# Carried state multiplied without a block copy, two more units with an early bonus, and a new order of all steps

## The chip, the cores and the metric

The kernel runs on one core of one Trainium2 chip. The metric is the device time of one execution in microseconds (us); the median of several runs counts. The core's engines are TensorE (PE in the profile; its weight loads are PEld), VectorE (DVE), ScalarE (ACT) and GpSimd (POOL); SyncE (SP) issues the DMAs.

## The reference

Three stages follow one another. A recurrence over time for 4 batches and 8 heads with a state of 48x48, then a feed-forward block with a softmax-weighted hidden layer and a layer norm, then a gated feed-forward block:

```python
for t in range(S):                       # B=4, H=8, S=768, D=48
    cur = einsum('bhd,bhe->bhde', u[None] * kt, vt)
    y[:, :, t] = einsum('bhd,bhde->bhe', rt, state + cur)
    state = wt[:, :, :, None] * state + einsum('bhd,bhe->bhde', kt, vt)
...
h = x @ w_in                             # 3072 x 384 -> 1024
e = exp(h - max(h)); solu = h * e / (sum(e) + 1e-9)
ln = (solu - mean(solu)) / sqrt(var(solu) + 1e-6) * g_ln
x = ln @ w_out                           # 1024 -> 384
...
gate = 1 / (1 + exp(-(x @ w_gate))); val = x @ w_val   # 384 -> 1536
out = (gate * val) @ w_out2              # 1536 -> 384
```

## The kernel before

**Units.** The recurrence is cut in 24 units, 6 chunks of 128 time steps for each batch. Within a unit the running product of the decay w (two scans, `sn1` and `sn2`, with the turn `cl` between them) scales r and k in place (`qm0`, `qm1`); `q` is the tile of scaled r and k. Then PE makes the scores of the chunk (`sco`, tile `pa`), a masked copy puts them into `a` (`mk0`, `mk1`) over a diagonal that holds the bonus term r·(u k) (`dg0`, `dg1` on POOL). The unit's output is two products that add up in one PSUM tile `py` (`out`): `a` times `v`, and the scaled r times the state that is carried in. The state is `yd` = old state + k·v (`new`, PE, then `yd`, DVE) and `xd` = `yd` times the decay `sc` (`scp` and `xd`). The first unit of a batch has no carried state, so 20 units have the second product. In the kernel before, `xb0` and `xb1` copy the two halves of `xd` into the tile `xblk`, whose other blocks stay zero, and the second product takes `xblk` as its weights, over all 112 rows.

**The bonus.** For units 0 to 2 it is one product in the layout of the scores (`rkp`) and four small matmuls against `u_blk` (`eb`, `ebc`). For the other units, r and k are loaded a second time in natural layout (`rk`), multiplied on POOL or DVE (`ru0`, `ru1`) and summed on DVE (`bon`).

**The feed-forward stages.** `g1a` to `g1c` are the first matmul of a unit (tile `ph`), `mx`, `ex`, `he`, `vs`, `rs0`, `rs1`, `no` the softmax and the norm, `zt` the transposes, `zh` and `zl` a high and a low part of the result, `g2` the second matmul (12 records a step; two steps a block of 128 columns for a pair of units), `xc` its copy. `g3g`, `g3v`, `ga`, `gm`, `gh`, `gl2`, `g4` are the gated block, whose PE work fills the time from about 385 us on. Weights arrive as 64-bit words and are decoded on DVE (`ci`, `co`, `wd`), with range watches on ACT (`ciw`, `cow`, `ww`); for units 0 to 2 the first matmul uses the plain decoded tile, from unit 3 on a high and a low part (`cih`, `cil`, `coh`, `col`).

**What sets the order.** The steps stand in a table, `ORDER`, in the order in which they are issued; each engine runs its own instructions in that order, and waits where data or a buffer is late. A suffix a, v or p puts a step on ACT, DVE or POOL. SP issues all loads in the table's order as well.

```python
    def step(name):
        name, _, at_ = name.partition(".")
        by = dict(by=at_[-1]) if at_[-1] in engines else {}
        ops[name](*map(int, at_.strip("avp").split(":")), **by)
```

Of the kernel before, what the change touches and what calls it, by code (L numbers as in the profile page):

```python
# [38 lines left out]
w.0 q.0 id.0 w.1 ub.0 mk.0 in_.0 q.1 sn1.0 v.0 in_.1 wo.0 cl.0 rkp.0p u.0 sn2.0 gl.0 q.2 qm0.0p in_.2 eb.0:0 v.1 v.2 ebc.0v sn1.1 qm1.0p sq.0 dg0.0  # L39
ktr.0:1 kcp.0 dg1.0 ciw.0 scp.1v cl.1 sco.0:2:3 w.2 ci0.0 sn2.1 rkp.1p q.3 new.0:4 eb.1:0 mk1.0 qm1.1p ebc.1 rk.3 sq.1 yd.0 mk0.0 dg0.1 ci1.0 out.0:1  # L40
dg1.1 ciw.1 ci0.1 v.3 ci1.1 xy.0 ci2.0 xm.0 qm0.1 cih.0 xd.0 ktr.1:0 ci2.1 xb1.0a kcp.1 sco.1:3:4 cow.0 cil.0v wo.1 mk0.1 rkp.2p mk1.1 cih.1 co0.0
eb.2:2 cow.1 co0.1 rk.4 cil.1v co1.0 ebc.2 ciw.2 dg0.2 new.1:1 dg1.2 yd.1 co2.0 ci0.2 cog.0 sn1.2 xb0.0 coh.0 out.1:0 ci1.2 scp.2 qm0.2p w.3 xy.1 v.4
ru0.3 q.4 g1a.0 xd.1 xm.1 ru1.3 cl.2 xb1.1a xb0.1 ci2.2 g1b.0 sn2.2 cih.2 g1c.0 cil.2v qm1.2p sq.2 cow.2 sco.2:3:4 mx.0 ru0.4 ktr.2:2 mk1.2 ex.0 ru1.4
mk0.2 sn1.3 out.2:1 kcp.2 rs0.0 cow.3 he.0 scp.3 new.2:0 qm0.3p w.4 v.5 xy.2 bon.3 q.5 g1a.1 vs.0 cl.3 xm.2 dg0.3 co1.1 dg1.3 rk.5 rs1.0 g1b.1 sn2.3
no.0 g1c.1 co0.2 qm1.3p sq.3 bon.4 zt1.0:4 co1.2 dg1.4 rk.6 zt0.0:3 zh1.0 ktr.3:2 zh0.0 dg0.4 sco.3:1:4 kcp.3 sn1.4 cl.4 scp.4 qm0.4p w.5 mx.1 sn2.4
ex.1 ru0.5v qm1.4p sq.4 yd.2 new.3:3 he.1 ru1.5 sco.4:2:0 rs0.1 xd.2 vs.1 g1a.2 ru0.6 mk1.3 yd.3 xb0.2 rs1.1 xb1.2a mk0.3 ktr.4:4 xd.3 g1b.2 kcp.4
ru1.6 co2.1 xb1.3a xb0.3 no.1 wl.0 new.4:3 sn1.5 out.3:1 cog.1 co0.3 qm0.5p coh.1 bon.5 v.6 xy.3 zt0.1:4 co1.3 dg1.5 rk.7 g1c.2 zh0.1 xm.3 dg0.5 scp.5
co2.2 g2.0 w.6 q.6 co2.3 cog.2 col.0v col.1 zt1.1:1 coh.2 cog.3 col.2 cl.5 zh1.1 ww.0 g2.1 mk0.4 sn2.5 mk1.4 qm1.5p xc.0 bon.6 out.4:4 sq.5 yd.4 rk.8
ru0.7v xd.4 ru1.7 coh.3 w.7 sn1.6 v.7 sco.5:1:2 xb1.4a xy.4 dg0.6 q.7 xm.4 dg1.6 g2.2 col.3 cl.6 g2.3 mx.2 qm0.6p sn2.6 ex.2 ru0.8v rs0.2 sq.6 qm1.6p
he.2 xc.1 g2.4 ru1.8 sn1.7 vs.2 ktr.6:0 wl.1 rs1.2 g2.5 kcp.6 mk0.5 xb0.4v scp.7 no.2 bon.7 qm0.7p w.8 mk1.5 rk.9 sco.6:3:4 xh.3 wd0.0 xc.2 xl.3  # L50
new.6:0 xh.4 out.5:1 mk1.6 xl.4 yd.6 xd.6 mk0.6 xy.5 dg1.7 q.8 zt1.2:2 cl.7 v.8 g1a.3 zh1.2 dg0.7 xm.5 xb1.6a ww.1 sn2.7 g1b.3 q.9 sn1.8 qm1.7p g1c.3
ru0.9 sq.7 ktr.7:4 mx.3 ru1.9 zt0.2:0 kcp.7 zh0.2 sco.7:3:1 scp.8 zl1.2 ex.3 qm0.8p w.9 zl0.2 out.6:4 mk0.7 xh.5 rs0.3 xb0.6 he.3 xl.5 new.7:2 xy.6
v.9 wd1.0 xm.6 vs.3 g1a.4 yd.7 rs1.3 bon.8 g1b.4 xd.7 rk.10 dg0.8 sn1.9 xb0.7 no.3 g1c.4 dg1.8 xb1.7a zt0.3:0 mx.4 xh.6 qm0.9p zt1.3:3 zh0.3 zh1.3
zl0.3 xl.6 ex.4 cl.8 g2.6 ru0.10 zl1.3 he.4 scp.9 g2.7 ru1.10 sn2.8 vs.4 g1a.5 wd2.0 qm1.8p xc.3 sq.8 g2.8 w.10 ktr.8:4 cl.9 wh.0 g1b.5 sn2.9 kcp.8
rs0.4v g2.9 qm1.9p sq.9 mk1.7 bon.9 bon.10 rs1.4 rk.11 ktr.9:2 xc.4 wlo.0 g1c.5 rk.12 kcp.9 no.4 g2.10 sn1.10 zt1.4:0 cl.10 scp.10 zt0.4:3 w.11 zh1.4
mx.5 ru0.11 g2.11 zh0.4 zl1.4 ru1.11 ex.5 sn2.10 sco.8:4:1 ru0.12 xc.5 new.8:2 ru1.12 out.7:0 he.5 rs0.5 sq.10 dg1.9 q.10 mk0.8 v.10 vs.5 g1a.6 dg0.9
wd0.1 xy.7 zl0.4 rs1.5 g1b.6 xm.7 yd.8 bon.11 no.5 sn1.11 g1c.6 rk.13 qm0.10p mk1.8 zt0.5:4 mx.6 zt1.5:0 zh0.5 sco.9:3:2 zh1.5 zl0.5 xh.7 wd1.1 ex.6
xl.7 new.9:1 out.8:4 rs0.6 ru0.13 he.6 xy.8 v.11 g2.12 dg1.10 q.11 xm.8 dg0.10 zl1.5 vs.6 g1a.7 cl.11 wd2.1 rs1.6 g2.13 no.6 qm1.10 g1b.7 mk0.9
qm0.11p xc.6 bon.12 xh.8 zt1.6:4 mk1.9 wh.1 rk.14 g2.14 xl.8 sn2.11 zh1.6 g1c.7 xd.8 qm1.11p sq.11 zl1.6 g2.15 wlo.1 xb0.8 scp.11 xb1.8a w.12 ru0.14
w.13 ktr.10:0 xc.7 zt0.6:3 g2.16 zh0.6 mx.7 zl0.6 ex.7 out.9:2 ru1.13v kcp.10v rs0.7 he.7 xy.9 dg1.11 q.12 sco.10:4:3 v.12 dg0.11 yd.9 vs.7 xm.9  # L60
sn1.12 new.10:0 sco.11:2:1 rs1.7 sn1.13 g1a.8 no.7 g2.17 qm0.12p mk0.10 mk1.10 cl.12 zt0.7:4 xc.8 sn2.12 g1b.8 zh0.7 mk1.11 qm1.12p sq.12 zt1.7:3
mk0.11 g1c.8 xd.9 zh1.7 xh.9v xb0.9 yd.10 xl.9 xb1.9a ktr.12:1 xd.10 kcp.12 out.10:2 mx.8 scp.13 xb1.10a w.14 xb0.10 ru1.14v ex.8 out.11:0 bon.13
dg0.12 q.13 zl1.7 rk.15 dg1.12 xy.10 v.13 he.8 rs0.8 xm.10 new.12:1 dg1.13 sco.12:3:2 zl0.7 dg0.13 vs.8 q.14 cl.13 v.14 g1a.9 sn2.13 q.15 rs1.8 g2.18
no.8 bon.14 qm1.13p sn1.14 rk.16 g1b.9 sq.13 ru0.15 xh.10 g2.19 ru1.15 yd.12 qm0.13 g1c.9 xl.10 xc.9 qm0.14p zt1.8:4 mk1.12 ktr.13:1 zh1.8 mx.9 g2.20
kcp.13 scp.14 ru0.16 w.15 mk0.12 ex.9 zt0.8:2 ru1.16 xd.12 g2.21 xb1.12a he.9 rs0.9 zh0.8 xb0.12 xc.10 new.13:1 cl.14 out.12:3 vs.9 sn2.14 rs1.9
bon.15 sq.14 v.15 g2.22 xy.11v rk.17 qm1.14p zl1.8 xm.11 no.9 zl0.8 g1a.10 sn1.15 dg1.14 xy.12 dg0.14 xm.12 zt1.9:0 zt0.9:4 g1b.10 zh0.9 qm0.15 scp.15
w.16 ru0.17 xh.11 g2.23 zl0.9 bon.16 ru1.17 cl.15 rk.18 g1c.10 xc.11 xl.11 zh1.9 sn2.15 g2.24 zl1.9 qm1.15p sq.15 mx.10 ktr.14:2 g2.25 kcp.14 ru0.18
sn1.16 ex.10 ktr.15:3 ru1.18 sco.13:4:0 kcp.15 xc.12 rs0.10 sco.14:2:3 cl.16 he.10 g2.26 xh.12v vs.10 xl.12v g1a.11 mk1.13 mk1.14 rs1.10 g2.27 yd.13
xd.13 no.10 sn2.16 scp.16 g1b.11 w.17 xb0.13 xc.13v sq.16 mk0.13 g1c.11 mk0.14 xb1.13 zt1.10:0 mx.11 g2.28 zh1.10 zl1.10 ex.11 zt0.10:3 sn1.17 g2.29
zh0.10 he.11 xc.14 new.14:1 zl0.10 out.13:4 vs.11 cl.17 sn2.17 out.14:2 xy.13 dg1.15 q.16 v.16 rs0.11v dg0.15 sq.17 yd.14 xm.13 xd.14 rs1.11 new.15:0  # L70
xy.14 xb1.14 v.17 sco.15:3:4 yd.15 dg0.16 no.11 q.17 xd.15 xm.14 dg1.16 g1a.12 xb0.14 xb1.15 scp.17 xb0.15 mk0.15 qm1.16p zt1.11:1 bon.17 xh.13
zt0.11:2 bon.18 rk.19 zh1.11 g1b.12 mk1.15 rk.20 zh0.11 zl1.11 zl0.11 g1c.12 qm1.17p qm0.16 g2.30 xh.14 qm0.17 w.18 mx.12 w.19 ktr.16:0 g2.31 xl.13v
xl.14 ex.12 kcp.16v sco.16:3:4 rs0.12 xc.15v he.12 g2.32 sn1.18 vs.12 g1a.13 sn1.19 rs1.12 g2.33 no.12 mk1.16 g1b.13 cl.18 xc.16 sn2.18 zt1.12:1
g1c.13 sq.18 cl.19 sn2.19 g2.34 mx.13 sq.19 zt0.12:2 mk0.16 ex.13 g2.35 ru0.19v ru0.20 zh0.12 rs0.13 he.13 xc.17 out.15:0 ru1.19 ru1.20v vs.13 zh1.12v
# [845 lines left out]
```

## Time and profile before

| | |
|---|---|
| median of 3 runs | 831.23 us (829.77 to 832.35) |
| the profiled execution | 830.05 us, its span 828.3 us |
| PE busy | 790.7 us, 95% of the span |
| DVE busy | 465.5 us, 56% |
| ACT busy | 350.4 us, 42% |
| POOL busy | 218.4 us, 26%, nearly all before 370 us |
| DMA | 62.69 MB, mean 76 GB/s |

Shares over the whole span hide the stages. The last 440 us are matmuls alone, back to back; DVE and POOL have nearly all their work for the recurrence in the first 290 us. So the page is read by stages, and a time is worth what it does to PE's idle time in its stage.

### The profile page before, as it was taken

The numbers are of one execution on the slowest core, as the hardware profiler recorded it, in microseconds if no ns is written. First come the engines' busy times: TensorE is split into PE (matmuls) and PEld (weight loads), VectorE is DVE, ScalarE is ACT, GpSimd is POOL, SyncE is SP. The second block draws the span as 40 slices with busy tenths as digits, with TensorE's granted clock in tenths as the row PEclk, the third lists the DMA queues.
The fourth block names the chain that finished last, engine by engine and source line by source line (L and its number), as shares of the span: only waits on it lengthen the run. The fifth ranks groups of instructions, "written<-read, shape, count | busy, mean of one in ns | idle before, by whom it ended". The sixth has DMA issues, their size and how long they took to land.

```text
span 828.3 us, 12255 instructions
## 1 busy us (share of the span) xinstructions
PE 790.7 (95%) x4904; PEld 658.9 (80%) x4904; DVE 465.5 (56%) x664; ACT 350.4 (42%) x594; POOL 218.4 (26%) x282
## 2 busy tenths in 40 slices
...
GB/s 307 301 117 157 213 89 137 100 184 86 153 120 143 49 44 7 130 45 133 268 1 5 34 1 0 39 1 0 1 39 1 0 35 5 0 1 39 0 1 42
DMA packets 21934, 62.69 MB, mean 76 GB/s; under 512 B 3440, under 2 KB 9456, under 8 KB 19696
## 3 DMA queue, kind: packets, MB, share of 16 engines
...
q14 instruction: 22, 0.18, 0.1%
q10 hardware_dynamic: 144, 0.13, 0.0%
...
## 4 chain that ended last, share of the span: by engine, by line
PE 74%; DVE 8%; POOL 7%; ACT 4%; DMA 3%; issue 3%; SPq 0%; POOLq 0%; DVEq 0%; ACTq 0%
PE pg L519 35%; PE p L546 18%; PE po L416 7%; PE ph L351 5%; PE py L300 3%; POOL q L206 2%; DMA w<-in_qw 2%; PE pa L270 2%; PE pz L393 2%; ACT e L387 1%; DVE e L365 1%; POOL st L381 1%; POOL a L250 1%; DVE w L192 1%; DMA xy<-xy 1%
## 5 line engine op out<-in xcount | busy, mean ns | idle before, releaser
L519 PE MATMUL pg<-xg,wj 128*128 128x512 f32 x1296 | 312.8, 394 | 0.0
L519 PEld LDWEIGHTS pg<-xg,wj 128*128 128x128 f32 x1296 | 242.7, 188 | 57.0
L526 DVE TENSOR_TENSOR sg<-pg,sg 128x512 f32<-128x512 f32 x72 | 49.7, 691 | 242.3 <-PE pg L519 217.9
L546 PE MATMUL p<-gv,wj 128*128 128x512 f32 x648 | 161.1, 394 | 0.0
L546 PEld LDWEIGHTS p<-gv,wj 128*128 128x128 f32 x648 | 121.7, 188 | 28.6
L523 ACT ACTIVATE sg<-pg 128x512 f32<-128x512 f32 x72 | 42.9, 597 | 180.4 <-PE pg L519 164.7
L416 PE MATMUL po<-zt,wo 128*128 128x256 f32 x792 | 107.7, 286 | 1.9 <-DVE zt L401 1.5
L416 PEld LDWEIGHTS po<-zt,wo 128*128 128x128 f32 x792 | 100.7, 190 | 7.2 <-DVE zt L401 2.1
L450 ACT CAST gv<-sg 128x512 fp32r<-128x512 f32 x72 | 44.6, 620 | 135.3 <-DVE sg L526 135.3
L351 PE MATMUL ph<-wi,xhl 128*128 128x512 f32 x378 | 97.1, 398 | 0.6 <-DVE e L365 0.6
L351 PEld LDWEIGHTS ph<-wi,xhl 128*128 128x128 f32 x378 | 67.6, 188 | 14.0 <-DVE e L365 0.7
L458 DVE TENSOR_TENSOR gv<-sg,gv 128x512 fp32r<-128x512 f32 x72 | 49.7, 691 | 45.7 <-ACT gv L450 45.6
L206 POOL TENSOR_TENSOR q<-q,w 112x512 f32<-112x512 f32 x37 | 50.0, 1356 | 14.8 <-DVE w L202 6.7
L250 POOL TENSOR_SCALAR_AFFINE_SELECT a<-bon 128x512 f32<-128x512 f32 x48 | 41.7, 890 | 24.5 <-PE py L300 17.7
L387 ACT ACTIVATE e<-e,st 128x1024 f32<-128x1024 f32 x24 | 29.8, 1243 | 39.3 <-POOL st L383 39.1
L356 DVE TENSOR_REDUCE st<-ph 128x1 f32<-128x1024 f32 x24 | 29.2, 1215 | 15.0 <-PE ph L351 13.9
L202 DVE TENSOR_TENSOR_SCAN w<-w,E 112x520 f32<-112x520 f32 x24 | 36.9, 1536 | 0.4
L192 DVE TENSOR_TENSOR_SCAN w<-w,E 112x520 f32<-112x520 f32 x24 | 32.4, 1359 | 6.7 <-DMA w<-in_qw 6.7
L273 DVE COPY_PREDICATED a<-msk,pa 128x512 f32<-128x512 uint32 x48 | 33.9, 731 | 2.0 <-PE pa L270 2.0
L370 ACT ACTIVATE scr<-e,st 128x1024 bf16<-128x1024 f32 x24 | 27.6, 1150 | 16.3 <-DVE st L366 15.8
L401 DVE TENSOR_TENSOR zt<-pz,zt 128x512 fp32r<-128x512 f32 x44 | 29.8, 682 | 7.7 <-ACT zt L450 7.4
L393 PE MATMUL pz<-idn,e 128*128 128x128 f32 x192 | 27.6, 275 | 5.7 <-ACT e L387 5.4
...
## 6 DMA issues: line engine op xcount, KB each, us to landing
...
x2T<-in_w_out SPq DMA_DIRECT2D x2, 1536.0 KB, 11.0
```

The lines of the kernel that those rows point to most:

```text
L192: nc.vector.tensor_tensor_scan(out=w, data0=w, data1=E.rearrange(flat), initial=0.0, op0=ALU.mult, op1=ALU.add)
L206: engines[by].tensor_tensor(out=q, in0=q, in1=w2_t[i][:, n, :, :, 0:64], op=ALU.mult)
L250: nc.gpsimd.affine_select(out=a_t[i].rearrange("p a h t -> p (a h) t")[:, :, c * 64:(c + 1) * 64], in_=bon_t[i].unsqueeze(2).to_broadcast( ...
L351: nc.tensor.matmul(ph[:, f * 512:(f + 1) * 512], xt[:, a, k, :], wi[:, b, k, f * 512:(f + 1) * 512], start=(k == n == 0), stop=(k == n == 2))
L393: nc.tensor.transpose(pz[:, j * P:(j + 1) * P], e_t[i][:, k * P:(k + 1) * P], idn)
L416: nc.tensor.matmul(po_t[n // 2], wo[:, a, k, dm * P:(dm + 1) * P], zt[:, b, k, cols[0]:cols[1]:cols[2], :], start=(k == m == 0), stop=(k = ...
L450: nc.scalar.copy(out, in_)
L458: engines[by].tensor_tensor(out=dst[:, 1], in0=src, in1=dst[:, 0].bitcast(F32), op=ALU.subtract)
L519: nc.tensor.matmul(pg, w[:, a, c:c + P], xt[:, b, k, :], start=(k == m == 0), stop=(k == m == 2))
L523: nc.scalar.activation(out=sg_t[n], in_=pp_t[n, 0], func=ACTF.Sigmoid)
L526: nc.vector.tensor_tensor(out=sg_t[n], in0=pp_t[n, 1], in1=sg_t[n], op=ALU.mult)
L546: nc.tensor.matmul(acc_t[g][d], w[:, a, c:c + P], gv[:, b], start=(j == 0 and m == 0), stop=(j == KJ - 1 and m == 2))
```

## The change

- The second product of `out` takes `xd` itself as its weights, for each head the 48 rows that it has (rows 0 to 47, or 64 to 111), and stands behind the product of `a` and `v` instead of ahead of it. The steps `xb0` and `xb1`, the two tiles `xblk` and their memsets are gone.
- Units 3 and 4 get their bonus as units 0 to 2 did: `rkp`, `eb`, `ebc` are there for five units, and `rk`, `ru0`, `ru1`, `bon` are gone for these two.
- The load of the first w is two DMAs of 520 columns instead of one of 1040.
- `ORDER` is a new table; in it, some steps change their engine: between the two tables POOL loses 5 of 37 scalings `qm`, 6 of 18 `scp`, and DVE gains these, 5 `xy`, 6 `xc` and 2 `zh` from ACT.

```diff
-    xblk = [xb_p.tile([ROWS, 4, ROWS], F32, name=f"xblk{i}") for i in range(2)]
...
-        nc.sync.dma_start(out=t, in_=qw[i][:, 1024:])
+        for a, e in ((0, 520), (520, 1040)) if i == 0 else ((0, 1040),):
+            nc.sync.dma_start(out=t[:, a:e], in_=qw[i][:, 1024 + a:1024 + e])
...
-        first = i % NC == 0
-        for n in range(1 if first else 0, 2):
+        parts = 1 if i % NC == 0 else 2
+        for n in range(parts):
             for hp in range(4):
                 for hh in range(2):
-                    m = D if hh else 64
-                    h = 2 * hp + hh
-                    if n == 0:
-                        lhs, rhs = xblk[i % 2][:, hp, 64 * hh:64 * hh + m], q[:, hp, 0::3, :]
+                    m = D if hh or n else 64
+                    h, r0 = 2 * hp + hh, 64 * hh
+                    if n:
+                        lhs, rhs = xd_t[i][r0:r0 + D, hp, :], q[r0:r0 + D, hp, 0::3, :]
                     else:
                         lhs, rhs = vv[:, h * D:h * D + m], a[:, hh, hp, :]
-                    nc.tensor.matmul(py[64 * hh:64 * hh + m, hp * P:(hp + 1) * P], lhs, rhs,
-                                     start=(hp == 0 and n == (1 if first else 0)), stop=(n == 1), skip_group_check=True)
+                    nc.tensor.matmul(py[r0:r0 + m, hp * P:(hp + 1) * P], lhs, rhs,
+                                     start=(hp == n == 0), stop=(n == parts - 1), skip_group_check=True)
...
-    def state_block(i, hh, by):
-        xd, xn, r0 = xd_t[i + 1], xblk[(i + 1) % 2], 64 * hh
-        copy(by, xn[r0:r0 + D, :, r0:r0 + D], xd[r0:r0 + D])
...
-... g1a.0 xd.1 xm.1 ru1.3 cl.2 xb1.1a xb0.1 ci2.2 g1b.0 sn2.2 cih.2 g1c.0 ...
+... g1a.0 cl.2 scp.2 qm0.2p sn2.2 xy.1 g1b.0 sq.1 xm.1 w.3 ci2.2 qm1.2p sq.2 rkp.3 g1c.0 cih.2 ...
```

How the table moves instructions is shown at two places. The first is DVE between two steps of the softmax, from `he` of unit 0 (L365 before, L359 after) to `mx` of unit 1 (TENSOR_REDUCE of `ph`). L192 and L202 are the scans, L196 and L197 the turn, L434 and L432 decodes, L243 the bonus sum. Before:

```order
L365 SCALAR_TENSOR_TENSOR e,st<-ph,e 128x1024
L366 TENSOR_SCALAR st<-st 128x1
L243 TENSOR_REDUCE bon<-rk 128x4x2
L196 TENSOR_SCALAR E_94<-w 112x8
L197 RECIPROCAL E_94<-E_94 112x8
L434 SCALAR_TENSOR_TENSOR raw_64<-x2T,raw_64 128x768
L202 SCALAR_TENSOR_TENSOR w<-w,E_94 112x520
L432 TENSOR_SCALAR e<-x2T 128x768
L243 TENSOR_REDUCE bon<-rk 128x4x2
L434 SCALAR_TENSOR_TENSOR e<-x2T,e 128x768
L192 SCALAR_TENSOR_TENSOR w<-w,E 112x520
L196 TENSOR_SCALAR E_94<-w 112x8
```

and after a second turn L197 comes L356, the `mx` of unit 1. In the change, at the same place:

```order
L359 SCALAR_TENSOR_TENSOR e,st<-ph,e 128x1024
L360 TENSOR_SCALAR st<-st 128x1
L190 SCALAR_TENSOR_TENSOR w<-w,E 112x520
L194 TENSOR_SCALAR E_94<-w 112x8
L195 RECIPROCAL E_94<-E_94 112x8
L200 SCALAR_TENSOR_TENSOR w<-w,E_94 112x520
L452 TENSOR_TENSOR wi<-spare_62,wi 128x1024
L426 TENSOR_SCALAR e<-x2T 128x768
L350 TENSOR_REDUCE st<-ph 128x1
```

Eleven instructions stood between the two steps, now six. The second place is POOL in the same stretch, around the three small steps of `rs1` of unit 0 (L381 to L383 before, L375 to L377 after). L250 is `dg`, L206 `qm`, L219 and L223 `ru0` and `ru1`. Before:

```order
L215 TENSOR_TENSOR sc<-w 112x4
L206 TENSOR_TENSOR q<-q,w 112x8x64
L250 AFFINE_SELECT a<-bon 128x8x64 x2
L381 TENSOR_SCALAR st<-st 128x1
L382 TENSOR_TENSOR st<-st,nhalf 128x1
L383 TENSOR_TENSOR st<-st 128x1
```

In the change:

```order
L248 AFFINE_SELECT a<-bon 128x8x64 x2
L369 TENSOR_SCALAR st<-st 128x1
L370 TENSOR_TENSOR st<-st 128x1
L217 TENSOR_TENSOR rk<-rk 128x384
L375 TENSOR_SCALAR st<-st 128x1
L376 TENSOR_TENSOR st<-st,nhalf 128x1
L377 TENSOR_TENSOR st<-st 128x1
```

The two `dg` and the `qm` that stood right ahead of `rs1` stand ahead of `rs0` or behind `rs1` now, and one `ru0` is between.

## Rows read from the trace of the kernel before

**Rows 1.** Stretches: busy us (x count) of PE, PEld, DVE, ACT, POOL; PEclk.

```profile
0.00:38.00 38.00, 19.05 (x145) 16.96 (x145) 30.48 (x35) 20.40 (x37) 19.88 (x27) 1.00 0.94 307
38.00:54.10 16.10, 14.98 (x94) 8.01 (x92) 14.91 (x21) 10.62 (x20) 13.77 (x12) 1.00 0.53 152
54.10:72.00 17.90, 14.55 (x109) 10.36 (x111) 16.48 (x23) 10.99 (x20) 15.65 (x18) 0.71 0.20 65
72.00:111.50 39.50, 35.57 (x295) 28.20 (x291) 33.49 (x46) 30.29 (x56) 35.77 (x38) 1.00 0.73 216
111.50:140.90 29.40, 27.98 (x261) 24.30 (x261) 27.46 (x39) 18.31 (x34) 20.01 (x26) 1.00 0.33 97
140.90:192.20 51.30, 50.80 (x469) 45.82 (x469) 47.25 (x70) 32.11 (x58) 40.71 (x52) 1.00 0.51 145
192.20:290.00 97.80, 95.60 (x944) 86.59 (x942) 89.61 (x151) 57.47 (x105) 52.34 (x76) 1.00 0.39 109
```

**Rows 2.** Timeline of PE up to 80 us: start, us, instruction.

```profile
9.26 1.84 PE L234 MATMUL pb<-u_blk,rk 112*128 112x2 f32 x8 [9.26 <-DMA u_blk<-in_u]
12.21 2.08 PE L270 MATMUL pa<-q 48*128 48x128 f32 x16
...
37.97 5.44 PE L345 MATMUL ph<-spare,xy 128*128 128x512 f32 x12
43.71 1.16 PE L270 MATMUL pa<-q 48*128 48x128 f32 x16 [0.30 <-POOL q L206]
...
48.63 5.39 PE L345 MATMUL ph<-spare,xy 128*128 128x512 f32 x12 [0.75 <-PE pk L283]
57.11 1.09 PE L393 MATMUL pz<-idn,e 128*128 128x128 f32 x8 [3.08 <-ACT e L387]
...
64.08 3.78 PE L345 MATMUL ph<-spare,xy 128*128 128x512 f32 x4
```

**Rows 3.** DVE groups by line from 0 to 39.6 us: busy, mean ns.

```profile
L202 DVE TENSOR_TENSOR_SCAN w<-w,E 112x520 f32<-112x520 f32 x3 | 6.5, 2178 | 0.0
...
L192 DVE TENSOR_TENSOR_SCAN w<-w,E 112x520 f32<-112x520 f32 x3 | 3.7, 1230 | 5.2 <-DMA w<-in_qw 5.2
...
L324 DVE TENSOR_TENSOR xd<-yd,sc 112x192 f32<-112x192 f32 x2 | 2.7, 1372 | 0.1
...
L458 DVE TENSOR_TENSOR wi<-spare,wi 128x1024 fp32r<-128x1024 f32 x2 | 2.4, 1214 | 0.0
...
L206 DVE TENSOR_TENSOR q<-q,w 112x512 f32<-112x512 f32 x1 | 0.7, 681 | 0.0
```

**Rows 4.** Timeline of DVE and POOL around the norm of unit 0.

```profile
47.32 1.20 DVE L365 SCALAR_TENSOR_TENSOR e<-ph,e 128x1024 f32<-128x1024 f32 x1
...
55.24 1.18 DVE L356 TENSOR_REDUCE st<-ph 128x1 f32<-128x1024 f32 x1
...
49.34 3.58 POOL L250 TENSOR_SCALAR_AFFINE_SELECT a<-bon 128x512 f32<-128x512 f32 x2 [0.51 <-DVE E L196]
52.91 1.96 POOL L381 TENSOR_SCALAR st<-st 128x1 f32<-128x1 f32 x1
```

**Rows 5.** One line's instructions: ns min/median/max.

```profile
L381 POOL TENSOR_SCALAR st<-st x24: 257/330/1959, 52.9 to 364.4; 128x1 f32<-128x1 f32 x24
```

**Rows 6.** Groups by line over the span: busy, mean ns.

```profile
L450 ACT COPY xblk<-xd 48x192 f32<-48x192 f32 x32 | 11.0, 347 | 4.1 <-DVE xd L324 3.8
...
L452 DVE COPY xblk<-xd 48x192 f32<-48x192 f32 x8 | 3.5, 435 | 0.2
```

**Rows 7.** Timeline of PE late in the recurrence.

```profile
311.37 1.09 PE L300 MATMUL py<-q,xblk 112*64 112x128 f32 x16
312.29 1.04 PE L300 MATMUL py<-a,v 128*48 128x128 f32 x16
...
322.09 1.16 PE L270 MATMUL pa<-q 48*128 48x128 f32 x16
323.18 1.70 PE L416 MATMUL po<-zt,wo 128*128 128x256 f32 x12
```

129 lines of the change are left out of this document (63 added, 66 removed).

## The prediction

> **What bounds the kernel now.** I read first the busy time by stretches, then the chain of waits on PE in the first 80 us. After 111.5 us PE is the bound: in the three stretches up to 290 us it is busy for 27.98 of 29.40, 50.80 of 51.30 and 95.60 of 97.80 us [rows 1], so all that it still loses there is 4.1 us, and behind that it only multiplies. What it loses before 111.5 us is 18.95 + 1.12 + 3.35 + 3.93 = 27.4 us of idle time, and more by its clock. The reader should see that in the same stretches DVE is nearly as full: 14.91 of 16.10, 16.48 of 17.90, 33.49 of 39.50, and later 27.46 of 29.40 and 47.25 of 51.30 [rows 1]. So the time is decided by how soon DVE hands PE its work before 111.5 us, and whether DVE keeps up after it.
>
> **Two more things are in the rows.** The 16 score matmuls of a unit took 2.08 us at 12.21 and 1.16 us at 43.71 [rows 2]: PE ran at its lower level (1.2 GHz) at first. The granted clock is 0.71 from 54.1 to 72 us [rows 1], so about 10 of these 17.9 us were again at 1.2 of 2.4 GHz, and a wait of 3.08 us of PE for ACT stands just ahead of it (the transposes at 57.11) [rows 2]. And DVE and POOL hold each other up: one and the same instruction on one column took POOL 257 ns at best and 1959 ns at worst [rows 5], that worst one at 52.91 [rows 4]; in the first 39.6 us the second scans took 2178 ns in the mean and the first scans, of the same shape, 1230 ns, and the two `xd` 1372 ns [rows 3] for 192 columns.
>
> **The early stage, step by step.** First w: its halves land sooner than the whole, which DVE waited 5.2 us for [rows 3], at most some 2 us sooner (half of it). I cost that at nothing: PE's first matmul waits until 9.26 for the u_blk load [rows 2], which stands at the same place of SP's queue, and the diagonals and masks of unit 0 stand behind it. Without that cover it would be worth up to 2 us.
>
> GEMM1 of unit 0 needs the last decode (`ci2.2`). Up to it, DVE does three `qm` (0.68 each [rows 3]), two decodes of w_out, a cast and the second scan of unit 2 (1.23 if alone) more: 2.0 + 1.9 + 0.5 + 1.2 = 5.6 us; and two `cil` (1.21 each [rows 3]), one `xd` (1.37), a `yd`, a `scp` and an `ebc` less: 2.4 + 1.4 + 0.9 = 4.7 us (the small ones and the decodes are estimates from like widths). That is 0.9 us more work. Against it, POOL runs fewer instructions beside DVE (two `qm` and more go). Of the 2.9 us that three second scans and of the 2 us that two `xd` lost to POOL I take back about half, 2 us, and 2 us of the 7.5 us that DVE stood idle before 38 us [rows 1], since the decodes of w_out now fill its waits. So GEMM1 of unit 0 can end about 3 us sooner than its 43.41 (37.97 + 5.44 [rows 2]), between 0 and 5: at 40.2.
>
> From there to GEMM1 of unit 1: scores of unit 2, their two masks, `rkp.4`, then `he.0`. The bonus matmuls of unit 3 stand in PE's way now, half of 1.84 us at the full clock [rows 2]; and the watch of w_out's second half stands ahead of `ex.0` on ACT. So I leave 1.7 of the 3 us: 46.9 for 48.63 [rows 2].
>
> From `he.0` at 47.32 to `mx.1` at 55.24 [rows 4] DVE did eleven instructions, 6.6 us. Six are left: scan 1.2, turn 0.4, scan 1.2 to 1.7, `cil` 1.2, decode 0.5, some 4.8 us. `mx.1` then waits for PE alone, GEMM1 of unit 1 (46.9 + 5.4 = 52.3), 2.9 us sooner than before. `rs1.0` stood behind two diagonals of 3.58 us on POOL and took 1.96 us itself [rows 4]; these two are out of its way, so the norm and the transposes of unit 0 come at about 53 and not 57.11. With `mx`, `ex` and `he` of unit 1 at 52.3 + 1.2 + 2.7 (`ex` behind two copies) + 1.3, GEMM1 of unit 2 starts at 57.9 and not 64.08 [rows 2]: **6.2 us gained**, with as many steps of PE ahead of it as before (27 and 27). The bounds are 2 (the start gains nothing, only the stretch from `he.0` on) and 9 (the start gains 5).
>
> From GEMM1 of unit 2 to the first GEMM2 of split weights (111.5 us) DVE has 52 steps before and 53 now, POOL 37 and 33, ACT 48 and 35, PE 34 and 35. DVE is full there, so I let it take the same 47.4 us; the 6.2 us stay.
>
> **What the rest takes back.** The carried-state product: before, `py` had two rounds of 16 records at 312.29 - 311.37 = 0.92 us each; the score matmuls, the only ones here that use two row halves of the array at once, took 323.18 - 322.09 = 1.09 us [rows 7]. The new product does both, halves by row and by column. It is the same 128 columns streamed, so I give it no gain; at worst it is the score row, 0.17 more. I take 0.1, half way, times 15 units behind 111.5 us: 1.5 us, from 0 to 2.6. The Trainium skill, "TensorEngine Tiling (Array Packing)", Key Properties, says that a change of the tiling mode drains the engine; the product adds such a change per unit. It names no price; the score row has such changes on both sides, so its 0.17 us is what the trace allows for it. By the rule alone the term would be the upper end.
>
> The state copies: ACT loses 32 of 347 ns, DVE 8 of 435 ns [rows 6]. ACT is not on the path (57.47 of 97.80 us [rows 1]), so that gives nothing; without that slack it would be 11 us of work. DVE gets more than it loses: from 111.5 to about 290 us 222 steps become 234 (five `xy`, six `xc`, six `scp`, four `zh`, two `qm` come, seven copies and some `ru`, `xh`, `xl` go), about 8 us by the mean of each. DVE is idle for 1.94 + 4.05 + 8.19 = 14.2 us there [rows 1], so 8 fit, but not in each place: from 140.9 to 192.2 us only 4.05 us are free and 7 of the 8 fall there. I take 1.0 us; nothing if POOL, which has less to do there, leaves DVE alone; all of 6.2 us if DVE becomes the bound. Two more `eb` are in the early stage's times; PE's other steps stand 0.6 us later against that point.
>
> Sum, against the profiled execution's 830.05 us: -6.2 + 0.6 + 1.5 + 1.0 = -3.1, so 826.95. That execution is 1.18 us under the median 831.23; the same difference on the median gives **828.1 us**.
>
> **The rivals.** About 0.3%, 2.5 us, is what a measurement of this kernel can tell from no change: 828.7 to 833.7 is "same".
> - Forecast: the early gain of 2 to 9 us survives in part. Its own range is 823 to 828.7. Chance 0.42.
> - More: POOL and DVE meet so seldom that DVE also runs ahead later, and PE loses none of its 4.1 us behind 111.5: -9 + 2 - 2 = -9, 822 us, down to 818. For it: scans, `xd` and turns lose time to POOL in every stretch. Against it: PE has little left to win. Chance 0.10.
> - DVE gives it back: the 8 us more of DVE work between 111.5 and 290 us bind, or PE's clock falls again in the fifties, which costs about half of the 10 us that it lasted. -6.2 + 2.1 + 4 to 6 = 830 to 833. For it: 47.25 of 51.30 us. Chance 0.28.
> - Slower, one mechanism: the matmuls of the two row halves write one PSUM bank, and are made to wait for each other. Then each product takes two rounds, 0.92 us more; 20 of them are 18.4 us, 15 behind 111.5 us 13.8: 828.1 + 13.8 - 1.5 = 840 us. It decides from 0.3 us a product on (15 x 0.3 = 4.5 against 4.6). For it: the score matmuls use two banks, one for each half, and no row shows two halves in one. Against it: the halves go to different partitions. Chance 0.07. The Trainium skill, same page, Gotcha 1, says it outright: different row tiles cannot use one PSUM bank at the same time; no row here shows it.
> - Slower through a new wait: the second half of w_out is loaded after the two first decodes of w_in, later by some 4 us than before, and its watch on ACT stands ahead of `ex.0`. If it lands some 5 us late, `he.0` and GEMM1 of unit 1 go with it, and 6.2 becomes -1 to -4: 834 to 837. It decides from 3 us late on. Chance 0.13.
>
> Range for 8 in 10: the last two hold 0.20 and the case "more" 0.10. I leave out the row-half case and parts of the outer two: 820 to 835. Faster: 0.42 and 0.10, 0.52 less a little that falls inside; same: the third and this, 0.29; slower 0.20.
>
> **What would show each step.** GEMM1 of units 0, 1 and 2 starting near 35, 47 and 58 us; the granted clock at 1.00 from 40 us on; second scans and `xd` nearer to 1.23 and 0.35 us; the second round of `py` at 0.9 to 1.1 us; DVE idle of 4 to 8 us between 111.5 and 290 us with PE's idle still near 4 us. I am wrong if GEMM1 of unit 2 starts after 62 us, if PE's idle behind 111.5 us grows by more than 3 us, or if the round of `py` takes 1.8 us.

## The result and the profile after

The changed kernel takes **837.48 us** in the median of 4 runs (836.31 to 838.79), the kernel before 831.05 (829.77 to 832.35): the ratio is 1.0076, with a 95% interval from 1.0060 to 1.0092. It is 6.4 us slower, where 2.9 us faster was forecast with a range from 820 to 835. The profiled execution took 837.13 us, its span is 835.1 us. PE is busy for 796.1 us (790.7 before), DVE for 469.0, ACT for 335.4, POOL for 209.7.

First the stretches of the kernel after; the columns are those of [rows 1]. The second begins with GEMM1 of unit 2 and ends at the first GEMM2 of split weights (tile `po` from `zt` and `wo`).

```profile
0.00:38.00 38.00, 19.61 (x144) 16.86 (x144) 28.01 (x36) 19.53 (x36) 12.54 (x22) 1.00 0.88 272
...
62.09:115.77 53.68, 45.62 (x357) 34.61 (x357) 49.84 (x64) 31.25 (x53) 42.87 (x45) 0.94 0.57 170
...
115.80:146.60 30.80, 29.52 (x281) 25.50 (x279) 28.25 (x40) 20.52 (x37) 27.47 (x29) 1.00 0.41 116
146.60:197.00 50.40, 48.23 (x462) 42.43 (x462) 47.06 (x77) 28.09 (x46) 41.47 (x48) 1.00 0.47 135
197.00:290.00 93.00, 92.66 (x839) 82.81 (x838) 81.90 (x139) 46.10 (x78) 47.79 (x69) 1.00 0.37 103
```

The same second stretch in the kernel before, and two lines of its PE timeline:

```profile
64.08:111.53 47.45, 43.49 (x342) 32.68 (x340) 41.43 (x56) 33.64 (x61) 41.81 (x44) 0.95 0.62 183
...
111.53 0.38 PE L416 MATMUL po<-zt,wo 128*128 128x256 f32 x1 [0.30 <-ACT zt L450]
...
313.16 0.56 PE L283 MATMUL pk<-v,kt 128*48 128x48 f32 x15
```

Between 115.8 and 290 us PE is idle for 1.28 + 2.17 + 0.34 = 3.8 us, before for 4.1 us [rows 1]: in sum it waits no longer there. The time is lost ahead of it, and in the product's own rounds. PE's timeline shows both, early and late:

```profile
38.11 6.56 PE L339 MATMUL ph<-spare,xy 128*128 128x512 f32 x12
...
50.42 5.42 PE L339 MATMUL ph<-spare,xy 128*128 128x512 f32 x12
57.00 1.09 PE L387 MATMUL pz<-idn,e 128*128 128x128 f32 x8 [1.16 <-ACT e L381]
...
62.09 3.70 PE L339 MATMUL ph<-spare,xy 128*128 128x512 f32 x8 [0.56 <-DVE e L359]
...
70.15 1.09 PE L387 MATMUL pz<-idn,e 128*128 128x128 f32 x8 [3.77 <-ACT e L381]
71.08 3.54 PE L339 MATMUL ph<-spare,xy 128*128 128x512 f32 x4
...
105.39 0.60 PE L255 MATMUL pt<-idn,q 112*128 112x112 f32 x4 [1.70 <-POOL q L204]
...
111.84 1.75 PE L387 MATMUL pz<-idn,e 128*128 128x128 f32 x8 [1.98 <-ACT e L381]
113.24 2.69 PE L345 MATMUL ph<-wi,xhl 128*128 128x512 f32 x6
115.77 1.48 PE L410 MATMUL po<-zt,wo 128*128 128x256 f32 x11
...
216.67 1.09 PE L298 MATMUL py<-a,v 128*64 128x128 f32 x16
217.69 1.08 PE L298 MATMUL py<-q,xd 48*48 48x128 f32 x16
218.69 1.09 PE L298 MATMUL py<-a,v 128*64 128x128 f32 x16
```

GEMM1 of unit 2 starts at 62.09 us, 2.0 us sooner than before and 4.2 us later than forecast. Then PE waits 3.77, 1.70 and 1.98 us, and behind the first and the last of these waits it runs at half rate: four matmuls take 3.54 us (8 take 3.70 at 62.09), eight transposes 1.75 us and not 1.09. The first GEMM2 of split weights starts at 115.77 us and not at 111.53. The rounds of `py` follow each other after 1.02 and 1.00 us, before after 0.92 and 0.87 [rows 7].

So the profiled span, 6.8 us longer (835.1 for 828.3), splits in two: 4.2 us are lost ahead of the first split GEMM2, and 2.6 behind it (719.3 for 716.8 us).

### The profile page after: what moved, and what is told of

Read it like the earlier page. It is cut to its first block, busy times and chain, and to the rows that moved or that the text cites. A ratio compares the mean times of both kernels' runs of the same rounds, so it can differ in the third digit from the quotient of the medians.

```text
span 835.1 us, 12250 instructions
## 1 busy us (share of the span) xinstructions
PE 796.1 (95%) x4920; PEld 659.6 (79%) x4920; DVE 469.0 (56%) x680; ACT 335.4 (40%) x549; POOL 209.7 (25%) x267
## 4 chain that ended last, share of the span: by engine, by line
PE 83%; DVE 5%; POOL 4%; DMA 3%; ACT 2%; issue 2%; SPq 1%; POOLq 0%; ACTq 0%; DVEq 0%
PE pg L513 36%; PE p L540 18%; PE po L410 10%; PE ph L345 7%; PE py L298 4%; PE pz L387 2%; PE pa L268 2%; DMA w<-in_qw 1%; PE ph L339 1%; POOL st L375 1%; PE po L406 1%; DVE w L200 1%; ACT e L381 1%; DVE a L271 1%; POOL st L376 1%
## 5 line engine op out<-in xcount | busy, mean ns | idle before, releaser
L410 PE MATMUL po<-zt,wo 128*128 128x256 f32 x792 | 106.6, 285 | 0.0
L345 PE MATMUL ph<-wi,xhl 128*128 128x512 f32 x378 | 99.4, 403 | 0.0
L204 POOL TENSOR_TENSOR q<-q,w 112x512 f32<-112x512 f32 x32 | 45.1, 1417 | 17.5 <-PE pz L387 6.0
L381 ACT ACTIVATE e<-e,st 128x1024 f32<-128x1024 f32 x24 | 29.8, 1243 | 45.0 <-POOL st L377 45.0
L248 POOL TENSOR_SCALAR_AFFINE_SELECT a<-bon 128x512 f32<-128x512 f32 x48 | 38.2, 811 | 36.4 <-PE py L298 24.4
L354 ACT ACTIVATE e<-ph,st 128x1024 f32<-128x1024 f32 x24 | 26.8, 1116 | 30.0 <-DVE st L350 30.0
L190 DVE TENSOR_TENSOR_SCAN w<-w,E 112x520 f32<-112x520 f32 x24 | 32.5, 1358 | 8.0 <-DMA w<-in_qw 8.0
L200 DVE TENSOR_TENSOR_SCAN w<-w,E 112x520 f32<-112x520 f32 x24 | 35.1, 1463 | 0.4
L387 PEld LDWEIGHTS pz<-idn,e 128*128 128x128 f32 x192 | 22.5, 143 | 15.4 <-ACT e L381 13.4
```

The costliest lines, as they stand in the source:

```text
L200: nc.vector.tensor_tensor_scan(out=w, data0=w, data1=E2.rearrange(flat), initial=0.0, op0=ALU.mult, op1=ALU.add)
L204: engines[by].tensor_tensor(out=q, in0=q, in1=w2_t[i][:, n, :, :, 0:64], op=ALU.mult)
L345: nc.tensor.matmul(ph[:, f * 512:(f + 1) * 512], xt[:, a, k, :], wi[:, b, k, f * 512:(f + 1) * 512], start=(k == n == 0), stop=(k == n == 2))
L387: nc.tensor.transpose(pz[:, j * P:(j + 1) * P], e_t[i][:, k * P:(k + 1) * P], idn)
L410: nc.tensor.matmul(po_t[n // 2], wo[:, a, k, dm * P:(dm + 1) * P], zt[:, b, k, cols[0]:cols[1]:cols[2], :], start=(k == m == 0), stop=(k = ...
```

## The experiments

Ratios are against the kernel before, run beside them, with their 95% intervals; the changed kernel stands at 1.0076 (1.0060 to 1.0092). Three theories were open: P, the product costs more; O, the new order loses; and later C, TensorE's clock.

### The parts one by one

**The product alone** (order, loads and bonus of before, without the steps `xb0` and `xb1`, the tiles `xblk` and their memsets):

```diff
+ lhs, rhs = xd_t[i][r0:r0 + D, hp, :], q[r0:r0 + D, hp, 0::3, :]
```

> The order and the loads of the kernel before, with the new product of the carried state alone: the scaled state is used directly, the block copies and their two tiles are gone. Two theories share the 6.4 us that the changed kernel lost. Theory P (the product): in the trace after, the step from the product's first record to the next work is 1.01 us where the kernel before had 0.92 and 0.87 for its rounds, about 0.2 us a unit with both changes of shape, 20 units, 15 of them behind 111.5 us where PE is the bound: 3 to 4 us slower than before, 834 to 835, with the spacings at 1.0 again. Theory O (the order alone lost it, and the product's longer spacing is hidden or is what any round costs next to other work): within 1 us of before, 830 to 832.

833.46 us (7 runs), ratio 1.0032 (1.0020 to 1.0044): 2.3 us slower in the medians. PE's timeline of this kernel, at the unit of [rows 7]:

```profile
313.47 1.09 PE L297 MATMUL py<-a,v 128*64 128x128 f32 x16
314.49 1.08 PE L297 MATMUL py<-q,xd 48*48 48x128 f32 x16
315.49 0.61 PE L280 MATMUL pk<-v,kt 128*64 128x48 f32 x15
```

Both rounds and the step to the next work are 315.49 - 313.47 = 2.02 us; before, the work behind the two rounds that start at 311.37 starts at 313.16, so 1.79. That is 0.23 us a unit and 3.5 us for the 15 units behind 111.5 us. P holds; the time shows 2.3 of the 3.5 us.

**The order with the old product** (block copies six steps behind each scaling, on ACT), here for the first unit:

```diff
- ... ci2.1 mk1.1 ...
+ ... ci2.1 xb0.0 xb1.0a mk1.1 ...
```

> The new order, split load and early bonus of the changed kernel, but with the old product: the block tiles, their clearing and the copies of the two halves are back, the copies on ScalarE a few steps behind each scaling. Theory P: the part of the 6.4 us that the product took comes back, 837.5 less 3 to 4, so 833.5 to 834.5; 2.9 us remain, which the order loses before the first GEMM2 of split weights. Theory O: it stays at 836.5 to 838.5. If the forecast's early gain were there and the product hid it, it would come out under 831.

839.32 us, from 835.65 to 844.32 in 6 runs, ratio 1.0093 (1.0068 to 1.0118). Neither theory expected it above the changed kernel. In the profiled execution, the slowest of the six, PE waited 2.00 us at 48.1 us for these copies, which stood behind an exponential on ACT: the edit brought a wait of its own, so it does not price the order. It shows no gain that the product hid, and cannot rule one out.

**The early bonus alone** (order and product of before), here for unit 3; unit 4 has the same:

```diff
- rk.3 ru0.3 ru1.3 bon.3
+ rkp.3p eb.3:1 ebc.3
```

> The order and the product of the kernel before, with the bonus of units 3 and 4 taken from the score layout: their second load of r and k, two products each on POOL and two sums on VectorE go, a product on POOL, four small matmuls and a copy on ScalarE come for each. Theory O says that the loss before 115 us lies in where the steps stand (q, w, ident and w_out late), not in the bonus: then this is at 830 to 832, or a little faster where POOL has less to do beside VectorE. A rival says that the small matmuls at PE's low clock (1.84 us for four) and their wait for POOL and ScalarE stand in the way of GEMM1: then 1.5 to 3 us slower, 833 to 834, and GEMM1 of unit 1 starts later than 49.5.

830.41 us (11 runs), ratio 0.9987 (0.9976 to 0.9997): 0.7 us faster in the medians. The bonus is not what lost; this is the only kernel of the study ahead of before, and by less than 0.3%. One sign of the rival is there all the same: in the profiled execution, the slowest of the eleven (832.83 us), GEMM1 of unit 1 starts at 50.40 us.

**The product twice:**

```diff
-        parts = 1 if i % NC == 0 else 2
+        parts = 1 if i % NC == 0 else 3
```

> The changed kernel with the product of the carried state done twice in each of the 20 units, one round right behind the other, so that the carried part of the output is doubled. If the longer spacing comes from the change between the two ways of using the array (128 rows, then two row halves, then 128 again), the second round, which follows one of its own kind, takes 0.85 to 0.93 us: about 18 us longer, 855 to 856. If the round is slow in itself, each takes 1.0: 20 us, 857 to 858. If the two row halves stood in each other's way, each would take 1.8.

One execution took 849.67 us, 12.2 us more than the changed kernel's median and not 18; 15 of the 20 second rounds stand behind the first split GEMM2, and 15 x 0.88 is 13.2. PE's timeline decides:

```profile
221.27 1.09 PE L298 MATMUL py<-a,v 128*64 128x128 f32 x16
222.29 1.95 PE L298 MATMUL py<-q,xd 48*48 48x128 f32 x32
224.17 1.09 PE L298 MATMUL py<-a,v 128*64 128x128 f32 x16
```

Two rounds take 1.88 us, one takes 1.00: the second, behind one of its own kind, costs 0.88, as a round did before (0.87 from 312.29 to 313.16). So the halves do not slow the product. The price sits at its two borders with the 128-row rounds, some 0.13 us each. The Trainium skill, "TensorEngine Tiling (Array Packing)", Key Properties, says that a change of the tiling mode drains the engine; that agrees, and these rows price it. The Trainium skill, same page, Gotcha 1, says that different row tiles cannot use a PSUM bank at once; if that made the halves wait for each other, each round would take about 1.8 us, an estimate from two rounds of 0.92. The rows don't show that.

### The order: one step moved, or half of it exchanged

DVE and POOL hold each other up here, as in [rows 4, 5]. The timeline of DVE and POOL after, at two places:

```profile
74.98 3.71 DVE L194 TENSOR_SCALAR E<-w 112x8 f32<-112x8 f32 x1
...
75.08 1.81 POOL L452 TENSOR_TENSOR wo<-raw,wo 128x768 fp32r<-128x768 f32 x1
76.85 1.81 POOL L452 TENSOR_TENSOR wo<-e,wo 128x768 fp32r<-128x768 f32 x1
...
106.54 1.94 DVE L428 SCALAR_TENSOR_TENSOR raw<-words,raw 128x1152 uint32<-128x1152 uint32 x1
...
107.24 2.37 POOL L375 TENSOR_SCALAR st<-st 128x1 f32<-128x1 f32 x1
```

At the first, the turn of eight columns on DVE takes 3.71 us (0.18 in the median) and ends at 78.69, when the two instructions on POOL are done (78.66). At the second, a norm's one column on POOL, begun during the decode on DVE, ends with the scan behind it (L190, to 109.62 us).

**The decode moved behind the norm of unit 3**, and **two products given back to POOL**:

```diff
- ... yd.6 wd1.0 kcp.7 ... zl0.3 zl1.3 dg1.8 ...
+ ... yd.6 kcp.7 ... zl0.3 zl1.3 wd1.0 dg1.8 ...
```

> The changed kernel with one step of the order moved: the second decode of the first block of gated weights on VectorE, which stands beside the norm of unit 3 on POOL, comes five steps of TensorE's later, behind the last low part of unit 3. In the trace after, the norm's first instruction took 2.37 us on one column beside this decode (1.94 us) and a scan, TensorE then waited 1.98 us for the normalised unit 3, and the granted clock fell to 0.58 behind it (8 transposes 1.75 and 6 matmuls 2.69 us instead of 1.03 and 1.55). Theory L (POOL is kept out by this one long instruction): the wait goes and the clock with it, 837.5 less 2.5 to 3.5, so 834 to 835. Rival: POOL waits for whichever VectorE instruction runs there, the next scan takes the decode's place, and the time stays at 836.5 to 838.

836.63 us, from 832.61 to 837.85, ratio 1.0071 (1.0054 to 1.0087): no gain that can be told from the changed kernel. PE's timeline of the profiled execution, which was the one of 832.61 us:

```profile
47.68 5.42 PE L339 MATMUL ph<-spare,xy 128*128 128x512 f32 x12
...
107.65 1.09 PE L387 MATMUL pz<-idn,e 128*128 128x128 f32 x8 [0.80 <-ACT e L381]
108.50 1.63 PE L345 MATMUL ph<-wi,xhl 128*128 128x512 f32 x6
109.97 2.31 PE L410 MATMUL po<-zt,wo 128*128 128x256 f32 x18
```

The wait for the normalised unit 3 shrank from 1.98 to 0.80 us and the half rate behind it is gone, as theory L had it. But of the 5.8 us that this execution is ahead at the first split GEMM2 (109.97 for 115.77) it has 2.7 already at GEMM1 of unit 1 (47.68 for 50.42), where its order is still that of the changed kernel.

```diff
- ru0.7v ru0.8v
+ ru0.7 ru0.8
```

> The changed kernel with the two products of r and k of units 7 and 8 on POOL again and not on VectorE, where they took 3.43 us between 92.6 and 96.1 us (0.60 us for the same product alone at 105.15) beside two diagonals and two other products on POOL. Theory L: VectorE is 3.4 us earlier with the scan, the maximum and the second scan behind them, POOL has 2 us more; the waits of TensorE for POOL's q (1.70 us at 105.39) and for the masks shrink, 1 to 3 us faster than the changed kernel, 834.5 to 836.5. Rival: POOL's 2 us more push the scaling that TensorE waits for at 105.39 by as much, 837.5 to 839.5.

837.43 us, ratio 1.0072 (1.0055 to 1.0090): no change that can be told. The wait for q at 106.6 us was 1.70 us again.

**The halves of the order exchanged** at the first third of GEMM1 of unit 3: one kernel has the order of before up to `g1a.3` and the new one behind it, the other the reverse.

> The order of the kernel before (with the early bonus for units 3 and 4 and the new product) up to the first third of GEMM1 of unit 3, which started at 96.7 us before and 92.9 us after; from there on the new order. Together with the next kernel it says in which half the new order loses. With the new product alone the kernel stood at 833.5, with the early bonus alone at -0.7 against before, so the old order throughout with both would be 832.8. Theory S (the new order's loss lies in its stretch from 93 to 116 us): 836 to 838 here. Rival (it lies in the start, where q, ident and w_out are loaded later): 832 to 833.5.

> The reverse: the new order with its split load up to the first third of GEMM1 of unit 3, and the order of before from there on; early bonus and new product as in the changed kernel. Theory S: the new start is some 1.7 us ahead at that matmul when the different work ahead of it is counted, and the old rest keeps it: 830.5 to 832. Rival (the new start loses): 836 to 838.

838.63 us, ratio 1.0095 (1.0079 to 1.0111), with the old start; 839.82, ratio 1.0111 (1.0091 to 1.0131), with the new one. Both medians are above those of either whole order, though the intervals overlap that of the changed kernel: the seam brought a wait of PE for POOL's q of 3.85 us at 107.1 us in the one, of 3.67 us at 102.7 us in the other. So these two say nothing about where the new order loses.

**The scaling of unit 1 ahead of the decodes**, alone and with the moved decode:

```diff
- sn2.1 cow.0 co0.0 ... co2.1 xy.0 ktr.0:0 qm1.1 ...
+ sn2.1 qm1.1 cow.0 co0.0 ... co2.1 xy.0 ktr.0:0 ...
```

> The changed kernel with one step moved: VectorE scales k and r of unit 1 (second half) ahead of the six first decodes of w_out, not behind them. In the trace after, that scaling met POOL's product of unit 2 at 22.1 to 24.7 us and took 1.75 us; VectorE then waited 1.33 us for the scores of unit 1, which stand behind it. In the profiled execution of the kernel with the later decode, whose order is the same up to there, VectorE was 0.4 us earlier, got ahead of POOL (0.68 us), the scores were in time, GEMM1 of unit 0 started at 36.5 in one piece and not at 38.1 in two, GEMM1 of unit 2 at 59.9 and not at 62.1, and the first GEMM2 of split weights at 110.0 and not at 115.8. Theory R (the new start hangs on this race, and loses it in most executions): moved ahead, the scaling takes 0.7 and the wait goes in each execution: 2.5 to 4.5 us faster than the changed kernel, 833 to 835. Rival (the start has slack up to the normalised units 0 and 1, or POOL meets a decode instead and all comes late again): 836.5 to 838.5.

> Both single moves in the changed kernel: the scaling of unit 1 ahead of the decodes of w_out, and the second decode of the first gated block behind unit 3's last low part. Theory R with L: 1 to 2 us below the kernel with the first move alone, 832 to 834, and the wait for the normalised unit 3 is under 1 us. Rival: no different from the first move alone.

The first alone: 837.15 us, ratio 1.0085 (1.0062 to 1.0108), no gain. With both: 834.75, ratio 1.0049 (1.0028 to 1.0069). Theory R falls by the profiles of the two: the scaling takes 0.69 us in each, DVE's times agree to 0.1 us from 13 to 42 us, PE is busy for 19.22 and 19.28 of the first 37 us, and still GEMM1 of unit 0 takes 7.47 us in the first kernel and 5.45 in the second. PE (PEld are its weight loads) in the first:

```profile
37.31 7.47 PE L339 MATMUL ph<-spare,xy 128*128 128x512 f32 x12
...
40.88 0.34 PEld L339 LDWEIGHTS ph<-spare,xy 128*128 128x128 f32 x1 [0.52 <-issue]
41.62 0.19 PEld L339 LDWEIGHTS ph<-spare,xy 128*128 128x128 f32 x1 [0.40 <-issue]
...
48.53 1.94 PE L298 MATMUL py<-a,v 128*48 128x128 f32 x14 [0.18 <-DVE a L271]
50.40 1.71 PE L298 MATMUL py<-q,xd 48*48 48x128 f32 x16
```

and in the second:

```profile
37.03 5.45 PE L339 MATMUL ph<-spare,xy 128*128 128x512 f32 x12
...
37.99 0.19 PEld L339 LDWEIGHTS ph<-spare,xy 128*128 128x128 f32 x1 [0.24 <-issue]
...
46.22 1.07 PE L298 MATMUL py<-a,v 128*48 128x128 f32 x14 [0.17 <-DVE a L271]
47.23 1.08 PE L298 MATMUL py<-q,xd 48*48 48x128 f32 x16
```

A load takes 0.34 us up to the one at 40.88 and 0.19 from 41.62 on in the first, 0.19 at 37.99 in the second: TensorE goes from 1.2 to 2.4 GHz at 41.6 us in the one and before 38 us in the other, with the same work done by then. The column of the granted clock says 1.00 in both there, so in the first 40 us the level has to be read from durations. GEMM1 of unit 1 follows at 52.03 and at 48.23. Of these 3.8 us, 0.3 are the later start of GEMM1 of unit 0 and 2.0 its late rise; 1.5 come from a second fall in the first kernel, behind a wait of 0.81 us at 47.9 us (granted 0.57 from 48 to 52 us; the two rounds take 1.94 and 1.71 us for 1.07 and 1.08). This is theory C.

**Both moves with the old product**, its copies right behind each scaling:

> The same two moves with the old product and its block copies, both on ScalarE right behind each scaling (and not six steps later, where they stood behind an exponential and TensorE waited 2.0 us for them at 48 us). Theory P (the product costs 0.23 us for each of 15 units that TensorE has no slack for, 3.5 us): 2.5 to 3.5 us below the kernel with both moves, 829 to 831, at or below the kernel before. Rival (ScalarE's copies come late in this order wherever they stand and give it back): 832 or more.

833.02 us in the median of 12 runs, ratio 1.0047 (1.0020 to 1.0073). The median is 1.7 us below that of the kernel with the new product, less than P expected, but two runs took 842, and the ratios of the two don't differ. Not settled by it.

### The waits filled

To take the clock's waits away, matmuls that nothing uses were put ahead of waits of PE, into a bank that is free at the time:

```diff
+    def warm(n):
+        pw, e = ps.tile([P, 512], F32, tag="o", name="pw", bufs=1), E.rearrange(flat)
+        for _ in range(n):
+            nc.tensor.matmul(pw[:, :2 * P], e[:, :P], e[:, P:3 * P])
...
+ wm.6 eb.0 ... wm.2 ktr.0 ... wm.4 ktr.1 ... wm.2 out.1 ... wm.2 zt0.0 ... wm.6 zt1.1 ... wm.3 ktr.7 ... wm.3 zt0.3
```

> The kernel before with 21 matmuls that nothing uses (112x128 by 256 columns, into a bank that is free until the first GEMM2) ahead of four of TensorE's waits before 58 us: 6 ahead of the first bonus, 4 ahead of unit 1's keys, 6 ahead of unit 1's output, 5 ahead of unit 0's transposes. Theory C (the clock is the large term of the early stage): before, the granted clock was 0.50 from 60 to 66 us behind a wait of 3.08 us, where the scores of units 3 and 4 took 2.1 us and not 1.16, and a third of GEMM1 of unit 2 3.8 us and not 1.9; without the fall the first split GEMM2 comes 3 to 5 us sooner than 111.5, and the time is 826 to 828.5. Rival (VectorE and POOL set the stage, the clock only fills the slack behind them, or the filling stands in the way): 830.5 to 833.

> The changed kernel with 28 such matmuls ahead of eight waits (6, 2, 4, 2, 2, 6, 3 and 3, the last two at 105 and 112 us). Theory C: GEMM1 of unit 0 takes 5.4 and not 6.6 to 7.5 us, the falls at 71 and 112 us go, 3 to 5 us faster than the changed kernel: 832.5 to 834.5; the 3.5 us of the product and the waits for VectorE and POOL stay. Rival: 836 to 838.5.

> The changed kernel with both moved steps (834.75 us in the median) and the same 28 matmuls. Its executions differ by 6 us, from 833.1 to 839.1. Theory C: that spread is the clock's; filled, the kernel comes out at 831.5 to 833.5 with a spread under 3 us. Rival: 834 to 836 with the same spread.

> The same with the old product and its block copies on ScalarE (833.0 us in the median, with single executions at 838 and 842). Theory C and P together: 828 to 830.5, 3 us below the kernel with the new product, and faster than the kernel before. Rival: 832.5 or more.

The kernel before, filled: 832.06 us, ratio 1.0000 (0.9987 to 1.0012). PE's timeline of it, with the scores as they were before (58.51) first:

```profile
58.51 2.19 PE L270 MATMUL pa<-q 48*128 48x128 f32 x16
...
59.18 1.27 PE L275 MATMUL pa<-q 48*128 48x128 f32 x16
...
63.93 3.54 PE L350 MATMUL ph<-spare,xy 128*128 128x512 f32 x4
...
112.80 0.38 PE L421 MATMUL po<-zt,wo 128*128 128x256 f32 x1 [0.30 <-ACT zt L455]
```

The scores at 59.18 take 1.27 us and not 2.19, but GEMM1 of unit 2 is no earlier (63.93 for 64.08), and the first split GEMM2 stands at 112.80 us. The time is as the rival has it: the half rate from 58 us on lay beside work that was late anyway. But the filling took only a part of the half rate away, since a third of GEMM1 of unit 2 still takes 3.54 us for 3.78 behind a wait of 1.70 that was not filled; what the clock costs the old order stays open.

The changed kernel, filled: 833.74 us (12 runs), ratio 1.0019 (1.0004 to 1.0034). That is 0.57% of 831, **4.7 us**, less than unfilled, give or take some 1.8 by the two intervals, as C expected. The stretch from GEMM1 of unit 2 to the first split GEMM2, and PE's timeline:

```profile
59.46:111.81 52.35, 48.15 (x380) 36.99 (x381) 50.33 (x64) 31.36 (x53) 42.72 (x45) 1.00 0.59 175
...
35.56 6.44 PE L344 MATMUL ph<-spare,xy 128*128 128x512 f32 x12
...
47.76 5.42 PE L344 MATMUL ph<-spare,xy 128*128 128x512 f32 x12
```

The clock no longer falls in this stretch, where the changed kernel has 0.94. The gain is all ahead of the first split GEMM2: 111.81 for 115.77, and 719.4 us behind it for 719.3. But 2.7 of these 4.0 us are there at GEMM1 of unit 1 (47.76 for 50.42), and the unfilled profile with the later decode was as early there (47.68); GEMM1 of unit 0 still takes 6.44 us, where C expected 5.4. The stretch itself only shrank from 53.68 to 52.35 us, with DVE as busy as before the filling. So the 4.7 us are what filling gives back; how much of them is the clock's fall, and how much a start that also differs between executions, is not separated.

With the two moved steps, filled: 833.64, ratio 1.0027 (1.0009 to 1.0045): no gain by the moves can be told once the waits are filled; the spread stayed (831.87 to 839.34), against C. With the old product, filled: 840.48, ratio 1.0099 (1.0086 to 1.0112), against C and P. PE's timeline of that one:

```profile
39.88 2.41 PE L352 MATMUL ph<-spare,xy 128*128 128x512 f32 x4 [2.26 <-DVE spare L444]
...
44.56 2.08 PE L276 MATMUL pa<-q 48*128 48x128 f32 x16
```

Two thirds of GEMM1 of unit 0 now ran at the full rate, PE then had to wait 2.26 us for the last decode, and behind that the scores took 2.08 us, half rate again. Three last kernels fill that wait too, or price the product with the waits filled:

```diff
+ wm.5 g1c.0 ... wm.3 out.6
```

> The new order with both moved steps, the old product and its copies, and the 28 unused matmuls as in the slow kernel, with 5 more ahead of the last third of GEMM1 of unit 0 and 3 more ahead of unit 6's output. Theory C (the slow filled kernel lost its time to the clock behind that one wait): the fall at 41 us goes and the time is 829 to 832, below the 833.0 of the same kernel unfilled. Rival (the copies on ScalarE are what is late in this order): 836 or more.

> The changed kernel with the 28 unused matmuls and the same 8 more. Without the 8 it stood at 833.7, with no fall of the clock behind 40 us in its profile: theory C expects 832.5 to 834 and a spread of 4 us or less; with theory P, 2 to 3.5 us above the kernel with the old product. Rival: the added matmuls stand in the way of GEMM1 of unit 0 and it is 835 or more.

> The order of before with the new product and the 21 unused matmuls; without the product's change that was 832.1. Theory P: 15 products behind 111.5 us at 0.23 each, 3.5 us, less what ScalarE's missing copies give: 834 to 835.5. Rival (part of the product's price is hidden by waits that it shortens, as the unfilled kernel's 2.3 us would say): 832.5 to 834.

The old product in the new order: 839.48 us, from 833.91 to 844.69, ratio 1.0114 (1.0084 to 1.0145). So filling the wait at 39.9 us did not make that kernel fast, against C. The changed kernel with more filling: 835.78, ratio 1.0050 (1.0032 to 1.0069), worse than with less; the rival holds in part: in its profile the added matmuls ahead of GEMM1's last third take from 41.65 to 43.81 us and that third starts behind them. GEMM1 of unit 0 was late already there (37.30 for 35.56 us) with the same work ahead of it. The product alone in the filled kernel before: 833.64, ratio 1.0029 (1.0014 to 1.0043) against 1.0000: 0.29%, 2.4 us, as without filling (0.32%). Its rival is right that about 1 us of the 3.5 is hidden.

## Why the prediction was wrong

The forecast's sum was -6.2 + 0.6 + 1.5 + 1.0 = -3.1; measured is +6.4. By the profiles, the part ahead of the first split GEMM2 was forecast at -6.2 and is +4.2; the part behind it was forecast at 0.6 + 1.5 + 1.0 = 3.1 and is +2.6. So what failed is the early gain. That the rest came out near is luck in part, since the product's own rounds ask for 3.5 us and not 1.5.

The rows for the second point below: DVE's waits in the first 38 us after (us in total, times, longest), and the last decode, before (L437) and after (L431).

```profile
DVE w L190 <- DMA w<-in_qw: 6.3, 2, 3.8
DVE q L204 <- POOL rk L227: 2.1, 1, 2.1
DVE a L271 <- PE pa L268: 1.3, 1, 1.3
...
38.36 1.18 DVE L437 SCALAR_TENSOR_TENSOR spare<-x2T,spare 128x1024 uint32<-128x1024 uint32 x1
...
40.08 1.19 DVE L431 SCALAR_TENSOR_TENSOR spare<-x2T,spare 128x1024 uint32<-128x1024 uint32 x1
```

- **The first load in two halves** at nothing: agrees. The first scan starts at 3.85 us, and PE's first matmul at 8.90 for 9.26 us [rows 2]. This part was not run alone.
- **GEMM1 of unit 0 3 us sooner: this step failed first.** It started at 38.11 us (37.97 before) and ended at 44.67, forecast 40.2. DVE was to use 2 us of its idle time; it is idle for 38 - 28.01 = 10.0 us in the first 38 us, and was for 7.5 us [rows 1]. Three waits make 9.7 of it: for two loads of w, for POOL's product of the early bonus, and for the scores of unit 1; before, two made 7.2. The last decode so ended at 41.27 us and before at 39.54: 1.7 us later and not sooner. Nor does GEMM1 wait for it in either kernel: the path that I took was wrong. And the first 2.5 us of GEMM1 ran at 1.2 GHz, which I had counted at the full rate because it was so before; it took 6.56 us for 5.44. GEMM1 of unit 1 came at 50.42 (forecast 46.9), of unit 2 at 62.09 (forecast 57.9): -2.0 and not -6.2. The transposes of unit 0 came at 57.00 and not at 53.
- **"The 6.2 us stay" up to the first split GEMM2: failed too.** I let DVE take the same 47.4 us; it took 53.68, and is busy for 49.84 us of them with 64 instructions, where it was for 41.43 with 56. Of these 8.4 us more, 5.0 are the turn's first instruction: five of them took 6.0 us (one 3.71, at 74.98), before three took 1.0; the products of r and k on DVE are another 2.6 (three took 4.0 us, before two 1.4). The 2.0 us ahead became 4.2 us behind (115.77 for 111.53), by waits of PE of 3.77, 1.70 and 1.98 us for chains through DVE and POOL, and by the clock behind them. I counted steps per engine there and took DVE's total as the time; that says nothing of single steps that exclude each other. The norm's first instruction, 257 to 1959 ns before [rows 5], took up to 2752 ns.
- **The product at 0.1 us a unit:** the mechanism was right, the size was not. It is 0.23 us, so 3.5 us by the rows and not 1.5; in the time of whole kernels of the old order it is 2.4 to 2.7 us. I took some half of the score row's 0.17 us and called 2.6 us the most that it could be; the two borders cost more than that row showed.
- **DVE's later 8 us at 1.0 us:** agrees, nearer to nothing, since PE's idle time behind 115.8 us is 3.8 us for 4.1.
- **The rivals.** "The clock falls again" was in the third one, at half of 10 us in the fifties; it fell at other places, and what it cost there by itself is not shown. The late second half of w_out did not decide; its price by its own terms is 828.1 + 6.2 + 1 to 4, so 835 to 838 and not 834 to 837. The serialised halves are refuted by the rounds of 0.88 us.

Of the 6.4 us, filling the waits gives back 4.7, and the product takes 2.4 to 2.7. What is left is about -0.8 us for the order, the split load and the bonus together, of which the bonus alone showed -0.7 to -1.1; it is by subtraction and smaller than the uncertainty of the 4.7. **Open** is what the new order gives with the old product: four such kernels ran from 832 to 845 us, and filling did not narrow that. Behind the first split GEMM2 their profiles take 719.4 to 725.2 us, none less than the 719.3 of the changed kernel, so that the product costs 2.4 us in the new order too is not shown. Open is also why the filled changed kernel still spreads by 6 us.
